# Trimming both ends of a tuned SwiGLU kernel: unread register setup, a one-column memset, 18 fillers for 20, and the last copy on ScalarE

## The chip, the cores and the metric

The kernel runs on one core of one Trainium2 chip. The metric is the device time of one execution in microseconds (us), lower is better. A run counts as slow when it is over 1.5% above the fastest run of the same kernel, and as fast otherwise; all quoted times are of fast runs unless a run is named as slow. The span in a profile is shorter than the time of the same run by 1.3 to 1.4 us; it counts from the first to the last recorded instruction.

## The reference

```python
B, S, D, F = 1, 2048, 640, 1536          # bf16 everywhere
def reference(x, w_gate, w_up, w_down):
    g = _silu(x @ w_gate)
    u = x @ w_up
    return (g * u) @ w_down
```

## The kernel before

The kernel cuts the 2048 rows into four blocks of 512. For each block it computes gate and up projections (tiles pg and pu) for 12 column groups, multiplies, and then computes the down projection in two tiles per 128 rows: po_a (512 columns) and po_b (128 columns). For the first block, x is loaded row by row and transposed on TensorE; the other blocks are loaded already transposed by DMA. While the first loads are under way, TensorE runs matmuls on a tile of ones whose result nobody reads. These are the "fillers"; they are meant to keep TensorE busy so that its clock goes to full rate early (how far these runs show it is asked under e4).

The head, with cuts marked:

```python
    ones = consts.tile([P, P], bf16)
    nc.vector.memset(ones[:], 1.0)
    queues = (nc.sync, nc.scalar)
    halves = ((0, KD // 2 + 1), (KD // 2 + 1, KD))
    for c in (0, 1):                      # x rows: chunks 0, 1 from SP, 2, 3 from ACT
        for i, eng in enumerate(queues):
            load_x(eng, c + 2 * i, c + 2 * i + 1)
    for dst, src in ((wg_sb, wg_v), (wu_sb, wu_v)):   # first 128 columns of both weights
        for eng, (k0, k1) in zip(queues, halves):
            eng.dma_start(out=dst[:, k0:k1, wslice(0, 1)], in_=src[:, k0:k1, wslice(0, 1)])
    # ... the other weights, then transposing loads of the later blocks
                h = (SUB - 1) * P
                warm(N_WARM)                          # N_WARM = 20
                for n, c in enumerate((0, 2, 1)):     # the "third chunk" below is c = 1
                    transpose_chunk(c, [(nc.vector.tensor_copy, ("po_a", "po_b")[n % 2], 0, KD)])
                transpose_chunk(SUB - 1, [...])
                warm(2)
                proj(pg, wg_sb, fc, sb, 0, h)         # first gate projection, 384 columns
                proj(pg, wg_sb, fc, sb, h, S_BLK)
                proj(pu, wu_sb, fc, sb, 0, S_BLK)     # first up projection
```

The tail, for the last 128 rows:

```python
            nc.scalar.copy(ot[:, 0:DA], po_a[:])
            # ... if last:
                nc.sync.dma_start(out=out2[s0 : s0 + P, 0:DA], in_=ot[:, 0:DA])      # 128 KB
                nc.vector.tensor_copy(out=ot[:, DA:D], in_=po_b[:])
                nc.scalar.dma_start(out=out2[s0 : s0 + P, DA:D], in_=ot[:, DA:D])    # 32 KB
```

After tracing, a function `_trim` takes barrier instructions out of the program's first block.

Of the kernel before, what the change touches and what calls it, by code (L numbers as in the profile page):

```python
# [10 lines left out]
def _body(  # L11
# [8 lines left out]
    nc = tc.nc  # L20
    P = nc.NUM_PARTITIONS
    f32 = mybir.dt.float32
    bf16 = mybir.dt.bfloat16
    ACT = mybir.ActivationFunctionType
    ALU = mybir.AluOpType

    B, S0, D = x.shape
# [8 lines left out]
    NSB = S // S_BLK  # L36
    SUB = S_BLK // P
    DA = 512
    N_WARM = 20
    W_CHUNKS = [(0, 1), (1, 3), (3, 6), (6, 9), (9, 12)]  # L40
    assert D % P == 0 and F % P == 0 and S % S_BLK == 0 and D > DA and SUB >= 2

    consts = ctx.enter_context(tc.tile_pool(name="consts", bufs=1))
# [25 lines left out]
    def load_w(eng, dst, src, a, b):  # L69
        eng.dma_start(out=dst[:, :, wslice(a, b)], in_=src[:, :, wslice(a, b)])  # L70
# [1 line left out]
    def load_x(eng, c0, c1):  # L72
        eng.dma_start(out=x_sb[:, c0:c1, :], in_=x_v[:, c0:c1, :])

    ones = consts.tile([P, P], bf16)
    silu_first = consts.tile([P, 1], f32)
    nc.vector.memset(ones[:], 1.0)  # L77

# [6 lines left out]
        for eng, (k0, k1) in zip(queues, halves):  # L85
            eng.dma_start(out=dst[:, k0:k1, wslice(0, 1)], in_=src[:, k0:k1, wslice(0, 1)])
    load_w(nc.sync, wg_sb, wg_v, *W_CHUNKS[1])
    nc.scalar.activation(silu_first[:], ones[:, 0:1], ACT.Silu)  # L88
    load_w(nc.sync, wu_sb, wu_v, *W_CHUNKS[1])
    for a, b in W_CHUNKS[2:]:  # L90
        load_w(nc.sync, wg_sb, wg_v, a, b)
# [6 lines left out]
    pw = psum.tile([P, S_BLK], f32, tag="gu", name="pw", bufs=4)  # L98

    def warm(n):  # L100
        for _ in range(n):
            nc.tensor.matmul(  # L102
                pw[:, 0:P], lhsT=ones[:], rhs=ones[:], start=True, stop=True
            )

    def keep_order(engine):
# [12 lines left out]
    def transpose_chunk(c, parts):  # L119
        c_sl = slice(c * P, (c + 1) * P)  # L120
        for copy, tag, k0, k1 in parts:
            pt = psum.tile([P, k1 - k0, P], bf16, tag=tag, name="pt")
            for kd in range(k0, k1):
                nc.tensor.transpose(  # L124
                    out=pt[:, kd - k0, :],
                    in_=x_sb[:, c, kd * P : (kd + 1) * P],
                    identity=ident[:],
                )
            copy(out=xT[:, k0:k1, c_sl], in_=pt[:])  # L129

    def proj(ps, w_sb, fc, sb, c0, c1):
        for kd in range(KD):
            nc.tensor.matmul(  # L133
                ps[:, c0:c1],
                lhsT=w_sb[:, kd, fc * P : (fc + 1) * P],
                rhs=xT[:, kd, sb * S_BLK + c0 : sb * S_BLK + c1],
                start=(kd == 0),
                stop=(kd == KD - 1),
            )

    for sb in range(NSB):
        s_sl = slice(sb * S_BLK, (sb + 1) * S_BLK)
        for fc in range(KF):
            pg = psum.tile([P, S_BLK], f32, tag="gu", name="pg", bufs=4)
            pu = psum.tile([P, S_BLK], f32, tag="gu", name="pu", bufs=4)
            if sb == 0 and fc == 0:
                h = (SUB - 1) * P
                warm(N_WARM)
                for n, c in enumerate((0, 2, 1)):
                    transpose_chunk(  # L150
                        c, [(nc.vector.tensor_copy, ("po_a", "po_b")[n % 2], 0, KD)]
                    )
                transpose_chunk(
                    SUB - 1,
                    [
                        (nc.vector.tensor_copy, "po_b", 0, 2),
                        (nc.scalar.copy, "po_a", 2, KD),
                    ],
                )
                warm(2)  # L160
                proj(pg, wg_sb, fc, sb, 0, h)
                proj(pg, wg_sb, fc, sb, h, S_BLK)
                proj(pu, wu_sb, fc, sb, 0, S_BLK)
                keep_order(mybir.EngineType.PE)
                keep_order(mybir.EngineType.Activation)
            else:
                proj(pg, wg_sb, fc, sb, 0, S_BLK)
                proj(pu, wu_sb, fc, sb, 0, S_BLK)
            sg = work.tile([P, S_BLK], f32)
            nc.scalar.activation(sg[:], pg[:], ACT.Silu)  # L170
            nc.vector.tensor_tensor(  # L171
                out=aT[:, fc, s_sl], in0=sg[:], in1=pu[:], op=ALU.mult
            )

        for j in range(SUB):
            s0 = sb * S_BLK + j * P
            last = sb == NSB - 1 and j == SUB - 1
            po_a = psum.tile([P, DA], f32, tag="po_a", name="po_a")
            for kf in range(KF):
                nc.tensor.matmul(  # L180
                    po_a[:],
                    lhsT=aT[:, kf, s0 : s0 + P],
                    rhs=wd_sb[:, kf, 0:DA],
                    start=(kf == 0),
                    stop=(kf == KF - 1),
                )
            po_b = psum.tile([P, D - DA], f32, tag="po_b", name="po_b")
            for kf in range(KF):
                nc.tensor.matmul(  # L189
                    po_b[:],  # L190
                    lhsT=aT[:, kf, s0 : s0 + P],
                    rhs=wd_sb[:, kf, DA:D],
                    start=(kf == 0),
                    stop=(kf == KF - 1),
                )
            ot = outp.tile([P, D], bf16)
            nc.scalar.copy(ot[:, 0:DA], po_a[:])  # L197
            if not last:
                nc.scalar.copy(ot[:, DA:D], po_b[:])  # L199
                nc.sync.dma_start(out=out2[s0 : s0 + P, :], in_=ot[:])  # L200
            else:
                nc.sync.dma_start(out=out2[s0 : s0 + P, 0:DA], in_=ot[:, 0:DA])
                nc.vector.tensor_copy(out=ot[:, DA:D], in_=po_b[:])  # L203
                nc.scalar.dma_start(out=out2[s0 : s0 + P, DA:D], in_=ot[:, DA:D])


def _trim(nc):







    blocks = nc.main_func.blocks
    main, end = blocks[0], blocks[-1]

    def of_barrier(ins):
        s = ins.sync_info
        if s is None:  # L220
            return isinstance(ins, mybir.InstDrain) and not ins.is_reset_sema
        names = [w.ant_name for w in s.on_wait] + [u.ant_name for u in s.on_update]
        return bool(names) and all(n.startswith("barrier_") for n in names)

    main.instructions[:] = [i for i in main.instructions if not of_barrier(i)]

    raised = {}
    for n, block in enumerate(blocks):
        for k, ins in enumerate(block.instructions):
            s = ins.sync_info  # L230
            for u in s.on_update if s is not None else []:
                raised[u.id] = (n, k)
    closing = []
    for ins in end.instructions:
        if of_barrier(ins):
            continue
        s = ins.sync_info
        if isinstance(ins, mybir.InstDrain) and s is not None and s.on_wait:
            waits = sorted(s.on_wait, key=lambda w: raised[w.id], reverse=True)
            closing.append(  # L240
                mybir.InstDrain(
                    name=ins.name,
                    engine=ins.engine,
                    is_reset_sema=ins.is_reset_sema,
                    debug=ins.debug,
                    sync_info=mybir.SyncInfo(on_wait=waits, on_update=list(s.on_update)),
                )
            )
        elif isinstance(ins, mybir.InstDrain) and ins.is_reset_sema:
            closing.append(  # L250
                mybir.InstDrain(
                    name=ins.name,
                    engine=mybir.EngineType.SP,
                    is_reset_sema=True,
                    reset_range_start=ins.reset_range_start,
                    reset_range_stop=ins.reset_range_stop,
                    debug=ins.debug,
                )
            )
        elif isinstance(ins, mybir.InstISA):  # L260
            closing.append(
                mybir.InstISA(
                    name=ins.name,
                    engine=mybir.EngineType.SP,
                    isa_opcode=ins.isa_opcode,
                    instr=list(ins.instr),
                    op_name=ins.op_name,
                    ant_dict=ins.ant_dict,
                    ant_isa_is_sequencer_only=ins.ant_isa_is_sequencer_only,
                    verify=ins.verify,  # L270
                    debug=ins.debug,
                    ins=[],
                    outs=[],
                )
            )
        else:
            closing.append(ins)
    end.instructions[:] = closing


def kernel(tc, *args):
    _body(tc, *args)
    tc.close()
    tc.compile()
    _trim(tc.nc)
# [30 lines left out]
```

## Time and profile before

| | before |
|---|---|
| time, median of 3 runs at first | 164.5 us (164.31 to 164.64) |
| span of the profiled run | 163.5 us |
| first gate projection starts | 5.08 us |
| first up projection starts | 6.54 us |
| TensorE's last signal to the end of the span | 2.08 us |

The first lines are from the page of the kernel before: the span, the busy time of each engine, and the chain of work that ended last, by engine.

```profile
span 163.5 us, 2138 instructions
PE 161.0 (98%) x911; PEld 81.3 (50%) x911; DVE 35.1 (21%) x54; ACT 44.0 (27%) x82; POOL 0.6 (0%) x6
...
PE 98%; DVE 0%; issue 0%; DVEq 0%
```

TensorE is busy 98% of the span and is 98% of the chain. What the change can reach are the few microseconds before the steady stream of matmuls and the two after it. The next lines are the timeline of the first 9 us of the same kernel. Columns: start, length, engine, source line, operation, output and inputs, number of instructions, and in brackets the idle time of the engine before it with what ended it. "PE" is a matmul on TensorE, "PEld" a weight load; further down "SPq" and "ACTq" are DMA issues.

```profile
start us, us, engine line op out<-in xcount [idle before <-releaser]
...
0.18 0.17 DVE L77 MEMSET ones<- 128x128 bf16 x1 [0.18 <-issue]
...
0.40 2.31 PE L102 MATMUL pw<-ones 128*128 128x128 bf16 x20 [0.40 <-DVE ones L77]
...
2.50 2.53 PE L124 MATMUL pt<-ident,x_sb 128*128 128x128 bf16 x20
...
3.28 1.02 DVE L129 COPY xT<-pt 128x640 bf16<-128x640 bf16 x2 [2.94 <-PE pt L124]
...
3.78 0.98 PEld L124 LDWEIGHTS <-x_sb 128*128 128x128 bf16 x10 [0.27 <-DMA x_sb<-in_x_dram]
...
4.54 0.69 DVE L129 COPY xT<-pt 128x640 bf16<-128x640 bf16 x2 [0.23 <-PE pt L124]
...
5.08 1.62 PE L133 MATMUL pg<-xT,wg_sb 128*128 128x384 bf16 x10
...
6.54 1.24 PE L133 MATMUL pu<-xT,wu_sb 128*128 128x512 bf16 x5
```

The reader should see three things. The fillers end where the transposes start, at 2.50. TensorE's weight load for the third x chunk waits 0.27 us for a DMA, until 3.78. The first gate projection starts at 5.08, just after the VectorE copy of the third chunk (the two copies from 4.54 on; the first of them ends near 5.03). The spacing of the 128x384 matmuls goes from 0.320 us to 0.163 us at 5.94: TensorE's clock goes from half rate to full rate there.

The DMA completions in the trace give the times at which the x chunks were there, in TensorE's order: 2.13, 2.62, 3.74 and 4.15 us. The first gate weights came in two halves, at 4.84 (SP) and 4.92 (ACT).

The tail of the same kernel, from the timeline:

```profile
160.80 0.58 ACT L197 CAST ot<-po_a 128x512 bf16<-128x512 f32 x1 [2.37 <-PE po_a L180]
161.41 0.33 SPq L202 DMA_DIRECT2D out_dram<-ot  x1
161.48 0.29 DVE L203 CAST ot<-po_b 128x128 bf16<-128x128 f32 x1 [12.34 <-PE po_b L189]
161.80 0.37 ACTq L204 DMA_DIRECT2D out_dram<-ot  x1
```

TensorE's last signal was at 161.40. VectorE starts the last copy 0.08 us later, and the last store is issued 0.40 us after the signal. It lands at 163.30, 1.50 us after its issue.

### The profile page before, as it was taken

The numbers are of one execution on the slowest core, as the hardware profiler recorded it, in microseconds if no ns is written. First come the engines' busy times: TensorE is split into PE (matmuls) and PEld (weight loads), VectorE is DVE, ScalarE is ACT, GpSimd is POOL, SyncE is SP. The second block draws the span as 40 slices with busy tenths as digits, with TensorE's granted clock in tenths as the row PEclk, the third lists the DMA queues.
The fourth block names the chain that finished last, engine by engine and source line by source line (L and its number), as shares of the span: only waits on it lengthen the run. The fifth ranks groups of instructions, "written<-read, shape, count | busy, mean of one in ns | idle before, by whom it ended". The sixth has DMA issues, their size and how long they took to land.

```text
span 163.5 us, 2138 instructions
## 1 busy us (share of the span) xinstructions
PE 161.0 (98%) x911; PEld 81.3 (50%) x911; DVE 35.1 (21%) x54; ACT 44.0 (27%) x82; POOL 0.6 (0%) x6
## 2 busy tenths in 40 slices
PE   9999999999999999999999999999999999999994
PEld 8644444455544444455554444445564444445552
DVE  2223333300013333310003333330001333331000
ACT  3222222222322222222232222222233222222321
POOL 1000000000000000000000000000000000000000
DMA  7999999611110000001210000001111000000112
GB/s 222 261 335 331 363 250 196 131 40 44 40 40 0 0 4 0 0 2 40 71 53 0 0 2 0 0 4 40 40 40 40 4 0 0 0 0 0 44 48 73
DMA packets 18953, 11.27 MB, mean 69 GB/s; under 512 B 9728, under 2 KB 18944, under 8 KB 18944
## 3 DMA queue, kind: packets, MB, share of 16 engines
q1 hardware_dynamic: 17968, 10.65, 23.1%
q10 hardware_dynamic: 976, 0.49, 1.1%
q8 instruction: 7, 0.11, 0.3%
q14 instruction: 2, 0.02, 0.0%
HBM read 6.55 MB, written 2.62 MB: 56 GB/s over the span
## 4 chain that ended last, share of the span: by engine, by line
PE 98%; DVE 0%; issue 0%; DVEq 0%
PE pg L133 32%; PE pu L133 32%; PE po_a L180 25%; PE po_b L189 7%; PE pw L102 2%; PE pt L124 1%; DVE ot L203 0%; DVE ones L77 0%; DVEq L203 0%
## 5 line engine op out<-in xcount | busy, mean ns | idle before, releaser
L133 PE MATMUL pg<-xT,wg_sb 128*128 128x512 bf16 (+2 forms) x245 | 60.0, 377 | 0.0
L133 PE MATMUL pu<-xT,wu_sb 128*128 128x512 bf16 x240 | 59.6, 379 | 0.0
L171 DVE TENSOR_TENSOR aT<-sg,pu 128x512 bf16<-128x512 f32 x48 | 33.0, 687 | 110.9 <-PE pu L133 110.9
L170 ACT ACTIVATE sg<-pg 128x512 f32<-128x512 f32 x48 | 28.7, 597 | 72.3 <-PE pg L133 72.3
L180 PE MATMUL po_a<-wd_sb,aT 128*128 128x512 bf16 x192 | 44.0, 379 | 0.0
L133 PEld LDWEIGHTS <-wg_sb 128*128 128x128 bf16 x245 | 23.9, 98 | 27.6 <-issue 0.3
L133 PEld LDWEIGHTS <-wu_sb 128*128 128x128 bf16 x240 | 23.4, 98 | 28.1
L180 PEld LDWEIGHTS <-aT 128*128 128x128 bf16 x192 | 18.3, 98 | 19.8
L197 ACT CAST ot<-po_a 128x512 bf16<-128x512 f32 x16 | 9.4, 585 | 40.4 <-PE po_a L180 40.4
L189 PEld LDWEIGHTS <-aT 128*128 128x128 bf16 x192 | 12.1, 98 | 3.8
L189 PE MATMUL po_b<-wd_sb,aT 128*128 128x128 bf16 x192 | 13.3, 219 | 0.0
L199 ACT CAST ot<-po_b 128x128 bf16<-128x128 f32 x15 | 4.0, 265 | 1.1
L102 PE MATMUL pw<-ones 128*128 128x128 bf16 x22 | 2.7, 313 | 0.4 <-DVE ones L77 0.4
L203 DVE CAST ot<-po_b 128x128 bf16<-128x128 f32 x1 | 0.3, 291 | 12.3 <-PE po_b L189 12.3
L124 PE MATMUL pt<-ident,x_sb 128*128 128x128 bf16 x20 | 2.5, 313 | 0.0
L102 PEld LDWEIGHTS <-ones 128*128 128x128 bf16 x22 | 2.3, 147 | 0.4 <-DVE ones L77 0.4
L129 DVE COPY xT<-pt 128x640 bf16<-128x640 bf16 (+1 forms) x4 | 1.7, 439 | 3.2 <-PE pt L124 3.2
L124 PEld LDWEIGHTS <-x_sb 128*128 128x128 bf16 x20 | 2.1, 146 | 0.3 <-DMA x_sb<-in_x_dram 0.3
L88 ACT ACT_TABLE_LOAD x1 | 1.3, 1283 | 2.0 <-issue 2.0
L129 ACT COPY xT<-pt 128x384 bf16<-128x384 bf16 x1 | 0.5, 478 | 1.5 <-PE pt L124 1.5
masks.py:199 POOL TENSOR_SCALAR_AFFINE_SELECT ident<-ident 128x128 bf16<-128x128 bf16 x1 | 0.3, 292 | 0.1
L88 ACT ACTIVATE silu_first<-ones 128x1 f32<-128x1 bf16 x1 | 0.2, 203 | 0.0
(6 smaller groups left out, 0.8 us busy)
## 6 DMA issues: line engine op xcount, KB each, us to landing
out_dram<-ot SPq DMA_DIRECT2D x15, 160.0 KB, 1.8
wd_sb<-in_w_down_dram SPq DMA_DIRECT2D x1, 1920.0 KB, 11.4
wg_sb<-in_w_gate_dram SPq DMA_DIRECT2D x3, 480.0 KB, 7.5
wu_sb<-in_w_up_dram SPq DMA_DIRECT2D x3, 480.0 KB, 7.6
x_sb<-in_x_dram SPq DMA_DIRECT2D x2, 160.0 KB, 2.7
x_sb<-in_x_dram ACTq DMA_DIRECT2D x2, 160.0 KB, 3.0
wg_sb<-in_w_gate_dram SPq DMA_DIRECT2D x1, 320.0 KB, 4.6
wu_sb<-in_w_up_dram SPq DMA_DIRECT2D x1, 320.0 KB, 5.1
```

The costliest lines, as they stand in the source:

```text
L88: nc.scalar.activation(silu_first[:], ones[:, 0:1], ACT.Silu)
L102: nc.tensor.matmul(pw[:, 0:P], lhsT=ones[:], rhs=ones[:], start=True, stop=True)
L124: nc.tensor.transpose(out=pt[:, kd - k0, :], in_=x_sb[:, c, kd * P : (kd + 1) * P], identity=ident[:],)
L129: copy(out=xT[:, k0:k1, c_sl], in_=pt[:])
L133: nc.tensor.matmul(ps[:, c0:c1], lhsT=w_sb[:, kd, fc * P : (fc + 1) * P], rhs=xT[:, kd, sb * S_BLK + c0 : sb * S_BLK + c1], start=(kd == 0 ...
L170: nc.scalar.activation(sg[:], pg[:], ACT.Silu)
L171: nc.vector.tensor_tensor(out=aT[:, fc, s_sl], in0=sg[:], in1=pu[:], op=ALU.mult)
L180: nc.tensor.matmul(po_a[:], lhsT=aT[:, kf, s0 : s0 + P], rhs=wd_sb[:, kf, 0:DA], start=(kf == 0), stop=(kf == KF - 1),)
L189: nc.tensor.matmul(po_b[:], lhsT=aT[:, kf, s0 : s0 + P], rhs=wd_sb[:, kf, DA:D], start=(kf == 0), stop=(kf == KF - 1),)
L197: nc.scalar.copy(ot[:, 0:DA], po_a[:])
L199: nc.scalar.copy(ot[:, DA:D], po_b[:])
L203: nc.vector.tensor_copy(out=ot[:, DA:D], in_=po_b[:])
```

## The change

The intent: let TensorE start earlier, because register moves whose value nobody reads no longer run ahead of the first memset on TensorE and VectorE, and the memset itself becomes short (one column, which the fillers then read 128 times over, with stride 0); take two fillers out, because the start is earlier; and let the last copy and its store sit on one engine.

```diff
@@ -36,7 +36,7 @@
     NSB = S // S_BLK
     SUB = S_BLK // P
     DA = 512
-    N_WARM = 20
+    N_WARM = 18
     W_CHUNKS = [(0, 1), (1, 3), (3, 6), (6, 9), (9, 12)]
     assert D % P == 0 and F % P == 0 and S % S_BLK == 0 and D > DA and SUB >= 2
 
@@ -72,7 +72,8 @@
     def load_x(eng, c0, c1):
         eng.dma_start(out=x_sb[:, c0:c1, :], in_=x_v[:, c0:c1, :])
 
-    ones = consts.tile([P, P], bf16)
+    ones = consts.tile([P, 1], bf16)
+    ones_p = ones[:].to_broadcast([P, P])
     silu_first = consts.tile([P, 1], f32)
     nc.vector.memset(ones[:], 1.0)
 
@@ -85,7 +86,7 @@
         for eng, (k0, k1) in zip(queues, halves):
             eng.dma_start(out=dst[:, k0:k1, wslice(0, 1)], in_=src[:, k0:k1, wslice(0, 1)])
     load_w(nc.sync, wg_sb, wg_v, *W_CHUNKS[1])
-    nc.scalar.activation(silu_first[:], ones[:, 0:1], ACT.Silu)
+    nc.scalar.activation(silu_first[:], ones[:], ACT.Silu)
     load_w(nc.sync, wu_sb, wu_v, *W_CHUNKS[1])
     for a, b in W_CHUNKS[2:]:
         load_w(nc.sync, wg_sb, wg_v, a, b)
@@ -100,7 +101,7 @@
     def warm(n):
         for _ in range(n):
             nc.tensor.matmul(
-                pw[:, 0:P], lhsT=ones[:], rhs=ones[:], start=True, stop=True
+                pw[:, 0:P], lhsT=ones_p, rhs=ones_p, start=True, stop=True
             )
 
     def keep_order(engine):
@@ -200,7 +201,7 @@
                 nc.sync.dma_start(out=out2[s0 : s0 + P, :], in_=ot[:])
             else:
                 nc.sync.dma_start(out=out2[s0 : s0 + P, 0:DA], in_=ot[:, 0:DA])
-                nc.vector.tensor_copy(out=ot[:, DA:D], in_=po_b[:])
+                nc.scalar.copy(ot[:, DA:D], po_b[:])
                 nc.scalar.dma_start(out=out2[s0 : s0 + P, DA:D], in_=ot[:, DA:D])
 
 
@@ -222,7 +223,23 @@
         names = [w.ant_name for w in s.on_wait] + [u.ant_name for u in s.on_update]
         return bool(names) and all(n.startswith("barrier_") for n in names)
 
-    main.instructions[:] = [i for i in main.instructions if not of_barrier(i)]
+
+    read = {
+        (i.engine, r) for b in blocks for i in b.instructions for r in i.regs_accessed()[0]
+    }
+    bare = (mybir.EngineType.PE, mybir.EngineType.DVE)
+
+    def idle_register(ins):
+        writes = ins.regs_accessed()[1]
+        return (
+            ins.engine in bare
+            and bool(writes)
+            and not any((ins.engine, r) in read for r in writes)
+        )
+
+    main.instructions[:] = [
+        i for i in main.instructions if not of_barrier(i) and not idle_register(i)
+    ]
 
     raised = {}
     for n, block in enumerate(blocks):
```

## The prediction

> **What bounds the kernel.** TensorE. The page gives PE 98% of a 163.5 us span; the chain of work that ended last is PE 98%, with everything else about 2%. The steady part (4 blocks of pg, pu, po_a, po_b) is not touched by the change. It can act only on the first 5 us and on the last 2 us.
>
> **Head, from the timeline of the first 7 us.** The VectorE memset of `ones` runs 0.18 to 0.34 us (165 ns). The first filler starts at 0.40; 20 fillers go about 107 ns apart; the first transpose starts at 2.50. The x chunks land (DMA completions) at 2.13, 2.62, 3.74 and 4.15 us in the order in which TensorE wants them. So TensorE does 10 transposes, sits idle 0.27 us until 3.78 (in the waits: weight load of x_sb on DMA), and only then goes on: the second half of the transposes, the last copies, the first real projection at 5.08. Chunk three's landing, not the fillers, sets 5.08. The clock gate opens inside the first projections: 128x384 matmuls are 320 ns apart at 5.36 and 163 ns from 5.94.
>
> **The change, part by part.**
> 1. Register setup. The two built programs, compared engine by engine, have no register move on TensorE or VectorE in either: the build already drops them. Apart from the memset the engines' preambles are the same. Gain 0.
> 2. One-column memset. Estimate from the trace: POOL's one-column memsets take 98 ns against 204 ns for 128x128, so VectorE's 165 ns may fall to about 70 to 100. The first filler starts near 0.30, 0.07 to 0.10 us earlier. Stride-0 reads of ones: I expect the same 107 ns spacing.
> 3. 18 fillers for 20: 2 x 107 = 0.21 us less. With 2 the first transpose starts near 2.2 instead of 2.50, just behind the chunk's landing at 2.13. The 10 transposes end 0.3 us earlier and the idle time before chunk three grows from 0.27 to about 0.55 us. First projection still at about 5.1. Gain about 0.
> 4. Last copy. Before: TensorE signals at 161.40, VectorE starts 80 ns later, takes 291, the ACT-issued store goes at 161.80 and lands at 163.30, closing the program. ScalarE is free at 161.39 and does this shape in 265 ns, starting about 67 ns after the signal (as its po_a copy did), and the store follows on the same engine. The store moves about 0.04 us earlier. Three waits of VectorE leave the program as well, off the path.
>
> **On the critical path:** 0.04 us in the tail, 0 to 0.1 us in the head.
>
> **The clock gate.** The Trainium skill, "TensorE: Matmul & The Clock Gate", Part 1, says that the half-rate state ends after a sustained busy window of about 3.4 us, free-running, so that the point varies from run to run. The trace agrees in kind: spacing halves 5.4 us after TensorE's first work. An earlier start shifts this by at most 0.1 us, worth half of that; random phase can move single runs by several tenths, about the scatter of before (164.31 to 164.64). The longer gap could delay the opening by a window, about 1.7 us lost (my estimate: half of 3.4); I give that 5%.
>
> **Prediction:** 164.4 us, range 164.0 to 164.8; within 2% nearly certain.
>
> **What would show it.** First filler near 0.30; spacing 107; first transpose near 2.2; idle before chunk three near 0.55 us; first projection within 0.2 us of 5.08; last ScalarE copy 265 ns; store issue about 0.35 us after TensorE's last signal instead of 0.40.
>
> **What would make it wrong.** Stride-0 operands read slower; the gate opening a window earlier or later; chunk three landing at another time, because TensorE no longer sets it but the queues do; the build dropping registers differently on the chip.

## The result, and the profile after

| | before | after |
|---|---|---|
| time, median | 164.57 us (164.31 to 164.93, 6 runs) | 164.79 us (164.49 to 165.13, 6 runs) |
| ratio of the fast runs | | 1.001, 95% interval 0.9991 to 1.003 |
| profiled span | 163.5 us | 163.6 us |
| first gate projection starts | 5.08 us | 5.60 us |
| first up projection starts | 6.54 us | 6.68 us |
| last signal to the end | 2.08 us | 2.09 us |

A ratio here is the mean time of one kernel's fast runs over the mean of the other's in the same rounds, so it is not quite the ratio of the medians. The two kernels cannot be told apart by time. The page after:

```profile
span 163.6 us, 2131 instructions
PE 160.1 (98%) x909; PEld 80.2 (49%) x909; DVE 34.8 (21%) x53; ACT 44.3 (27%) x83; POOL 0.6 (0%) x6
...
PE 96%; DMA 2%; DVE 0%; SPq 0%; ACT 0%; issue 0%
PE pg L134 32%; PE pu L134 32%; PE po_a L181 25%; PE po_b L190 7%; DMA x_sb<-in_x_dram 2%; DVE xT L130 0%; PE pt L125 0%; SPq L73 0%; ACT ot L204 0%
```

A DMA has entered the chain with 2%. The same places of the timeline as before:

```profile
0.15 0.06 DVE L78 MEMSET ones<- 128x1 bf16 x1 [0.15 <-issue]
...
0.30 2.10 PE L103 MATMUL pw<-ones 128*128 128x128 bf16 x18 [0.30 <-DVE ones L78]
...
2.50 1.25 PE L125 MATMUL pt<-ident,x_sb 128*128 128x128 bf16 x10
...
3.25 1.03 DVE L130 COPY xT<-pt 128x640 bf16<-128x640 bf16 x2 [3.04 <-PE pt L125]
...
4.56 0.73 PE L125 MATMUL pt<-ident,x_sb 128*128 128x128 bf16 x10 [0.81 <-DMA x_sb<-in_x_dram]
...
5.05 0.69 DVE L130 COPY xT<-pt 128x640 bf16<-128x640 bf16 x2 [0.77 <-PE pt L125]
...
5.60 1.25 PE L134 MATMUL pg<-xT,wg_sb 128*128 128x384 bf16 x10 [0.19 <-DVE xT L130]
...
6.68 1.24 PE L134 MATMUL pu<-xT,wu_sb 128*128 128x512 bf16 x5
```

And the part of the chain of waits, in order of time, that shows why (start, length, what):

```profile
0.45 4.06 DMA x_sb<-in_x_dram
...
4.56 0.47 PE pt L125 x5
...
5.60 1.25 PE pg L134 x10
```

The memset fell from 0.17 to 0.06 us and the first filler came at 0.30 instead of 0.40, as intended. Nothing came of it. The transposes started at 2.50 again, now held by the landing of the first chunk (2.45) and not by the fillers. The third chunk's load landed at 4.51, so TensorE sat idle for 0.81 us (1.13 us from one transpose to the next), and the first gate projection started 0.52 us later than in the profile of before. It then took only 1.09 us instead of 1.46, because the clock had already gone to full rate by 4.6 us. The sum, 0.52 - 0.37 = 0.14 us (rounded from the trace), is the whole difference at the first up projection.

The tail after:

```profile
160.94 0.59 ACT L198 CAST ot<-po_a 128x512 bf16<-128x512 f32 x1 [2.37 <-PE po_a L181]
161.55 0.33 SPq L203 DMA_DIRECT2D out_dram<-ot  x1
161.56 0.27 ACT L204 CAST ot<-po_b 128x128 bf16<-128x128 f32 x1
161.86 0.37 ACTq L205 DMA_DIRECT2D out_dram<-ot  x1
```

TensorE's last signal was at 161.54. The copy now starts 0.02 us after it and the store is issued 0.32 us after it, so 0.08 us earlier than before. Yet the end comes 2.09 us after the signal, against 2.08.

The three parts add up exactly in the two profiles: from the start of the first up projection to TensorE's last signal both take 154.858 us. So 163.48 = 6.54 + 154.86 + 2.08 and 163.63 = 6.68 + 154.86 + 2.09. The change does nothing in the middle; what it did at the two ends is what the experiments are about.

### The profile page after: what moved, and what is told of

The parts are those of the page before. It is cut to its first block, busy times and chain, and to the rows that moved or that the text cites. A ratio compares the mean times of both kernels' runs of the same rounds, so it can differ in the third digit from the quotient of the medians.

```text
span 163.6 us, 2131 instructions
## 1 busy us (share of the span) xinstructions
PE 160.1 (98%) x909; PEld 80.2 (49%) x909; DVE 34.8 (21%) x53; ACT 44.3 (27%) x83; POOL 0.6 (0%) x6
## 4 chain that ended last, share of the span: by engine, by line
PE 96%; DMA 2%; DVE 0%; SPq 0%; ACT 0%; issue 0%
PE pg L134 32%; PE pu L134 32%; PE po_a L181 25%; PE po_b L190 7%; DMA x_sb<-in_x_dram 2%; DVE xT L130 0%; PE pt L125 0%; SPq L73 0%; ACT ot L204 0%
## 5 line engine op out<-in xcount | busy, mean ns | idle before, releaser
L125 PE MATMUL pt<-ident,x_sb 128*128 128x128 bf16 x20 | 2.0, 266 | 0.9 <-DMA x_sb<-in_x_dram 0.8
L125 PEld LDWEIGHTS <-x_sb 128*128 128x128 bf16 x20 | 1.5, 120 | 1.4 <-DMA x_sb<-in_x_dram 1.4
```

Source lines behind the costliest of these rows:

```text
L125: nc.tensor.transpose(out=pt[:, kd - k0, :], in_=x_sb[:, c, kd * P : (kd + 1) * P], identity=ident[:],)
```

## The experiments

Theory: (1) the register edit removes nothing; (2) the head is set by when x chunks and first weights land and by when the clock opens, both of which differ from run to run and neither of which the change touches; (3) the tail gains a few hundredths of a microsecond at most. Rivals: the earlier start or the missing fillers cost something (a later clock); the change has a cost of its own of about 0.2 us; and for the tail, that ScalarE is in its own way.

Runs e1 to e4 were on one chip together, e5 to e8 on another, e9 to e11 on a third. Each group is compared with its own runs of the kernel before (of those with e9 to e11 one, 166.85 us, was slow and is not counted).

### e1_registers_only: the register edit alone

```diff
 (kernel before)
+    main.instructions[:] = [
+        i for i in main.instructions if not of_barrier(i) and not idle_register(i)
+    ]
```

> Only the register edit. The built program is the same as the kernel before's but for debug lines, so this is a run of before against itself. Theory (the register edit removes nothing): ratio 1.000, within 0.2% either way, memset at about 0.18 us and first filler at about 0.40 us; the spread of this ratio is the noise that every other ratio here has to beat. Rival (the edit removes register moves that the trace does not show): the memset starts clearly before 0.15 us and the time falls by 0.1 us or more.

Measured: 164.46 us (164.05 to 164.79, 6 runs) against 164.68 (164.23 to 165.42, 11 runs) of before; ratio 0.9985, interval 0.9961 to 1.0009. The built program is that of before, instruction for instruction: neither has a register move on TensorE or VectorE left, since the build drops them itself. In the profile the first filler is at 0.398 us, as in before. TensorE's timeline of this run:

```profile
0.40 2.31 PE L102 MATMUL pw<-ones 128*128 128x128 bf16 x20 [0.40 <-DVE ones L77]
2.50 1.94 PE L124 MATMUL pt<-ident,x_sb 128*128 128x128 bf16 x20
...
4.71 1.25 PE L133 MATMUL pg<-xT,wg_sb 128*128 128x384 bf16 x10 [0.16 <-DVE xT L129]
```

There is no wait for the third chunk: it landed at 3.46. The clock was at full rate from 3.57 us on, and the first up projection started at 5.80 us (its record is missing; this is the next one's 6.02 less one spacing of 0.216). That is 0.74 us earlier than in the other profile of the very same program. What follows: two profiles of one program differ at this point by more than the change was ever going to give, and a ratio of 0.15% off 1 with these counts is noise. The rival is out: the memset started no earlier.

### e2_tail_only: only the last copy on ScalarE

```diff
 (kernel before)
-                nc.vector.tensor_copy(out=ot[:, DA:D], in_=po_b[:])
+                nc.scalar.copy(ot[:, DA:D], po_b[:])
```

> Only the last copy on ScalarE. Theory: from the end of TensorE's last signal to the issue of the last store 0.40 us falls to 0.35 us or a little less, time -0.04 us, so ratio 0.9998, not to be told from 1. Rival (ScalarE is still busy with the po_a copy and delays it): the copy starts more than 0.1 us after the signal and the store leaves no earlier than before.

Measured: 164.74 us (164.35 to 165.05), ratio 0.9995, interval 0.997 to 1.0019. In the trace the copy starts 0.023 us after the signal and the store is issued 0.318 us after it, instead of 0.401. The gain at the issue is 0.08 us, twice the forecast. But the store landed 1.89 us after the signal, as before (1.90), and the span ended 2.06 us after it (2.08 before). The rival, that ScalarE delays the copy, is out. Where the 0.08 us went is asked in e9 to e11.

### e3_head_only: only the memset, the stride-0 ones and the 18 fillers

```diff
 (kernel before)
-    N_WARM = 20
+    N_WARM = 18
-    ones = consts.tile([P, P], bf16)
+    ones = consts.tile([P, 1], bf16)
+    ones_p = ones[:].to_broadcast([P, P])
 (and lhsT=ones_p, rhs=ones_p in warm)
```

> Only the one-column memset, stride-0 ones and 18 fillers. Theory (the landing of the x chunks and of the first gate weights sets the first projection, the fillers do not): first filler near 0.30, first projection between 5.0 and 5.7 us depending on when the last part of the third chunk lands, ratio 1.000 within 0.2%. Rival (fewer fillers open TensorE's clock later, which is what cost the 0.2 us): full-rate spacing is reached later than 5.9 us and the ratio is 1.001 to 1.005.

Measured: 164.76 us (164.38 to 166.32, 6 runs), ratio 1.0011, interval 0.9976 to 1.0046; one run of 166.32 makes the interval wide. In the profile the fillers run at the same 0.107 us spacing, the third chunk landed at 4.04, the first gate projection started at 5.38 and took 1.09 us; full-rate spacing was reached by 4.9 us. The rival said later than 5.9: in this it is wrong, and of the six other profiles with 18 fillers and the same head only e9 opens that late (table below). The theory's window for the start (5.0 to 5.7) holds.

### e4_no_fillers: the changed kernel with no filler ahead of the transposes

```diff
-                warm(N_WARM)
```

> The changed kernel without any filler ahead of the transposes. Theory (fillers do not gate the first projection, they only open the clock): first projection still between 5.0 and 5.7 us, but half-rate spacing lasts about 1 to 3 us longer, 0.5 to 1.5 us more in all (ratio 1.003 to 1.009). Rival (fillers are in the way of the transposes): the first projection comes earlier and the time falls. Rival 2 (fillers are useless, the transposes alone open the clock at the same point): ratio 1.000.

Measured: 165.13 us (164.46 to 166.13, 6 runs), ratio 1.0029, interval 0.9995 to 1.0063. TensorE's timeline:

```profile
2.46 2.32 PE L125 MATMUL pt<-ident,x_sb 128*128 128x128 bf16 x20 [2.46 <-DMA x_sb<-in_x_dram]
...
4.83 1.80 PE L134 MATMUL pg<-xT,wg_sb 128*128 128x384 bf16 x10
6.46 1.24 PE L134 MATMUL pu<-xT,wu_sb 128*128 128x512 bf16 x5
```

The first gate projection started at 4.83 us, a little before the theory's 5.0 to 5.7. Other profiles with fillers reach 4.71 to 4.94, so taking the fillers away does not bring it forward beyond them. It took 1.64 us instead of 1.09, because the clock opened only at about 6.0 us. The runs spread over 1.7 us, against 0.7 us in e1. The mean loss of 0.3% is in the direction of the theory, but the interval just includes none. So the fillers do not hold the start. That they do their work through the clock is not shown: with 20 fillers the clock opened at 5.94, 3.57 and 6.46 us, so 6.0 without any is inside what fillers give too, and what they are worth is not settled by these six runs and one profile.

### e5_fillers_40: the changed kernel with 40 fillers

```diff
-    N_WARM = 18
+    N_WARM = 40
```

> The changed kernel with 40 fillers ahead of the transposes. Theory (there is slack of about 1 us between the end of 18 fillers and the landing of the third chunk; beyond it fillers are on the path): the fillers run to about 4.0 to 4.6 us, the first projection starts at 5.3 to 6.5 instead of 4.7 to 5.6, most of the projections run at full rate from the start, so the time changes by +0.2 to +1.0 us (ratio 1.001 to 1.006). Rival (fillers are hidden however many): ratio 1.000, first projection at about 5.0.

Measured: 165.51 us (165.2 to 166.22, 4 runs), ratio 1.0054, interval 1.0032 to 1.0076.

```profile
0.31 4.10 PE L103 MATMUL pw<-ones 128*128 128x128 bf16 x40 [0.31 <-DVE ones L78]
4.25 1.35 PE L125 MATMUL pt<-ident,x_sb 128*128 128x128 bf16 x20
...
6.07 1.25 PE L134 MATMUL pg<-xT,wg_sb 128*128 128x384 bf16 x10 [0.35 <-DVE xT L130]
```

The transposes start at 4.25 instead of 2.5, the first gate projection at 6.07, as forecast. The 22 more fillers are on the path for part of their length. So there is a slack after 18 fillers, of the order of the wait for the third chunk, and it is not endless. Two fillers fewer, 0.21 us, lie inside that slack.

### e7_weights_before_x3: another order of the first loads

```diff
-    for c in (0, 1):
-        for i, eng in enumerate(queues):
-            load_x(eng, c + 2 * i, c + 2 * i + 1)
+    for eng, c in ((nc.sync, 0), (nc.scalar, 2), (nc.sync, 1)):
+        load_x(eng, c, c + 1)
 (first gate weights as before)
+        if n == 0:
+            load_x(nc.scalar, 3, 4)
 (the transposes of chunk 3 moved behind the first 384 columns of the gate projection,
  and the first up projection split into the same two parts)
```

> The changed kernel with the last x chunk issued behind the first gate weights and transposed after the first gate projection of 384 columns; the first up projection is split the same way. Theory (the first projection waits for DMA bandwidth: four x chunks and the first gate weights, 800 KB): 160 KB less ahead of it, so the first projection starts at about 4.4 to 4.7 instead of 4.7 to 5.6, and the second column of work ends 0 to 0.5 us earlier; ratio 0.997 to 1.000. Rival (a late part of one DMA engine sets it whatever the order): first projection no earlier than 5.0, ratio 1.000 or above for the extra instructions.

Measured: 165.18 us (164.5 to 166.56, 6 runs), ratio 1.004, interval 1.0006 to 1.0073: slower by 0.4%, and the expectation failed. The waits of TensorE (engine, line, what it waited for: us in total, times, longest):

```profile
...
PEld L135 <- DMA wg_sb<-in_w_gate_dram: 0.9, 1, 0.9
```

ACT's half of the first gate weights landed at 3.82 us, but SP's half landed at 5.31, later than the 4.5 to 4.9 of every other profile. The likely reason, not tested, is that SP's half still stands behind two x chunks in SP's queue, and that the moved chunk on ACT now shares the bandwidth with it. This order was a poor test of the bandwidth idea: if that is so, it took bytes from ahead of one half and put them beside the other. It does show that the first gate weights can hold the first projection as well as the third x chunk.

### e8_after_again: the changed kernel once more

No edit.

> The changed kernel itself once more. Theory (its 0.2 us over before was chance: the landing of the x chunks and the opening of the clock differ from run to run): ratio 0.998 to 1.001, the first up projection starts anywhere from 5.8 to 6.8 us, and from there to TensorE's last signal it takes 154.86 us as in every run so far. Rival (the change has a cost of its own): ratio 1.001 again or above.

Measured: 164.71 us (164.6 to 164.87, 5 runs), ratio 1.0001, interval 0.9987 to 1.0014. The 0.1% of the first measurement did not come back. One part of the expectation failed: from the first up projection (6.05 us, again one spacing ahead of the first record) to the last signal it took 155.29 us, not 154.86. The waits show where:

```profile
...
PEld L134 <- DMA wg_sb<-in_w_gate_dram: 1.1, 2, 0.8
...
PE pg L134 <- DMA wg_sb<-in_w_gate_dram: 0.3, 1, 0.3
```

With the first column group done early, TensorE stood 0.42 us before the second group, whose gate weights had not landed. The same stretch is longer in three more of the early ones, by 0.05 us in e6, 0.24 in e10 and 0.09 in e11, but not in e1. So behind the third x chunk and the first weights a third DMA is waiting to take over. An early first projection is then worth less than it seems.

### e6_tail_five_copies: is the last copy on the path?

```diff
-                nc.scalar.copy(ot[:, DA:D], po_b[:])
+                for _ in range(5):
+                    nc.scalar.copy(ot[:, DA:D], po_b[:])
```

> The changed kernel with the last 128x128 copy done five times over on ScalarE before its store (same result). Theory (the last copy is on the path one for one): four more copies of 0.265 us put the store 1.06 us later and the time rises by about 1.1 us, ratio 1.0065. Rival (the tail is set by the other store, or by the end of the program): less than half of that.

Measured: 165.65 us (165.54 to 166.04, 4 runs), ratio 1.0061, interval 1.0044 to 1.0077; e8 on the same chip had 164.71.

```profile
161.01 1.46 ACT L205 CAST ot<-po_b 128x128 bf16<-128x128 f32 x5
162.50 0.36 ACTq L206 DMA_DIRECT2D out_dram<-ot  x1
```

The store was issued 1.51 us after the signal instead of 0.32, so 1.19 us later, and the end came 3.16 us after the signal instead of 2.09: 1.07 us later. The copy is on the path, but 0.12 us of the delay cost nothing. That was the first hint that in the changed kernel the last store waits for something else for about a tenth of a microsecond.

### e9_no_big_store and e10_no_big_store_vector: what the last store waits for

Both give a wrong result: the 128 KB store of the last tile is left out.

```diff
 (e9: changed kernel)
-                nc.sync.dma_start(out=out2[s0 : s0 + P, 0:DA], in_=ot[:, 0:DA])
 (e10: also)
-                nc.scalar.copy(ot[:, DA:D], po_b[:])
+                nc.vector.tensor_copy(out=ot[:, DA:D], in_=po_b[:])
```

> Wrong result on purpose: the changed kernel without the 128 KB store of the last tile's first 512 columns. So far the last store was issued 0.08 us earlier with the copy on ScalarE (0.319 after TensorE's last signal against 0.401) but landed no earlier (1.89 to 1.91 against 1.90). Theory A (the last store's parts queue behind the 128 KB store on the same DMA engines, whose landing is 1.71 to 1.74 either way): without that store the last store lands about 1.5 us after its issue, 1.80 after the signal, and the program ends at about 1.98 instead of 2.06 to 2.11. Theory B (a store issued by ScalarE right after its own copy takes longer by itself): it still lands at about 1.9 and the end stays at 2.06 to 2.11.

> The same wrong-result kernel with the last copy on VectorE. Theory A: issue at 0.40, landing 1.88 to 1.90, end at about 2.06 to 2.08, so 0.08 later than with ScalarE: without the big store the earlier issue does count. Theory B: the same end as e9_no_big_store within 0.03 us.

The tails, e9 first and then e10 (start, length, engine and line, operation):

```profile
161.66 0.27 ACT L203 CAST ot<-po_b 128x128 bf16<-128x128 f32 x1
161.95 0.37 ACTq L204 DMA_DIRECT2D out_dram<-ot  x1
```

```profile
161.20 0.29 DVE L203 CAST ot<-po_b 128x128 bf16<-128x128 f32 x1 [12.34 <-PE po_b L190]
161.52 0.37 ACTq L204 DMA_DIRECT2D out_dram<-ot  x1
```

The trace's records of signals and DMA completions, all in us after TensorE's last signal:

| kernel | last copy on | last store issued | it landed | after its issue | 128 KB store landed | end |
|---|---|---|---|---|---|---|
| before | VectorE | 0.401 | 1.901 | 1.500 | 1.714 | 2.082 |
| e1, e3 | VectorE | 0.401, 0.402 | 1.897, 1.902 | 1.496, 1.500 | 1.710, 1.711 | 2.078, 2.078 |
| after | ScalarE | 0.319 | 1.908 | 1.589 | 1.737 | 2.088 |
| e2, e8 | ScalarE | 0.318, 0.319 | 1.891, 1.924 | 1.573, 1.605 | 1.720, 1.752 | 2.062, 2.094 |
| e9 | ScalarE | 0.317 | 1.808 | 1.491 | none | 1.989 |
| e10 | VectorE | 0.402 | 1.896 | 1.494 | none | 2.078 |

Without the big store the earlier issue counts in full: 1.989 against 2.078, 0.09 us. With it, the last store lands about 0.17 to 0.19 us after the big one whether it was issued at 0.32 or at 0.40. Theory A of the expectation holds, theory B does not. In the kernel before, the last store came just late enough not to be held at all (1.500 against 1.494 without the big store). The Trainium skill, "DMA: Bandwidth & Descriptors", section "Issuing engines are not separate DMA queues", says that transfers started from different engines run on the same 16 DMA engines and interleave. The table fits it: the last store, issued from another queue, is delayed by the big one by about 0.1 us here (1.573 to 1.605 after the issue against 1.491).

The times of these two kernels, 164.69 and 164.61 us with two runs each (ratios 1.0001 and 0.9996), decide nothing.

### e11_split_po_a: getting the big store out of the way

```diff
-            nc.scalar.copy(ot[:, 0:DA], po_a[:])
+            if not last:
+                nc.scalar.copy(ot[:, 0:DA], po_a[:])
+            else:
+                nc.scalar.copy(ot[:, 0 : DA // 2], po_a[:, 0 : DA // 2])
+                nc.vector.tensor_copy(out=ot[:, DA // 2 : DA], in_=po_a[:, DA // 2 : DA])
```

> Right result: the changed kernel with the last tile's 512-column copy split between ScalarE and VectorE, so that the 128 KB store is issued 0.15 to 0.25 us earlier. Theory A: the big store lands 0.15 to 0.25 us earlier, the last store no longer queues behind it, lands at about 1.80 after the signal, the end comes at about 1.98 instead of 2.08: 0.1 us, which the times (interval 0.15 to 0.25%) cannot resolve, ratio 0.9985 to 1.001. Theory B: the end stays at 2.06 to 2.11.

Measured: 164.98 us (164.78 to 165.35, 6 runs), ratio 1.0023, interval 1.0 to 1.0046. The edit did not do what it was for:

```profile
160.45 0.37 ACT L201 CAST ot<-po_a 128x256 bf16<-128x256 f32 x1 [2.37 <-PE po_a L181]
160.85 0.42 DVE L202 CAST ot<-po_a 128x256 bf16<-128x256 f32 x1 [12.06 <-ACT ot L201]
161.07 0.27 ACT L208 CAST ot<-po_b 128x128 bf16<-128x128 f32 x1 [0.25 <-PE po_b L190]
161.30 0.33 SPq L207 DMA_DIRECT2D out_dram<-ot  x1
161.37 0.37 ACTq L209 DMA_DIRECT2D out_dram<-ot  x1
```

The two half copies ran one after the other, because the program makes VectorE wait for ScalarE's copy into the same tile. The big store was therefore issued 0.25 us after the signal, 0.25 us later than before, while the last store was issued at 0.319 as in the changed kernel. The end moved from 2.09 to 2.34 us, by the same 0.25. So the run is a test of theory A after all, in the other direction: the big store moved, the last store's issue did not, and the end followed the big store. Its time missed the forecast too (0.9985 to 1.001), on the slow side. No version here beats both kernels; a version that gets the big store out earlier would gain about the 0.09 us of e9 (an estimate), less than these times can resolve.

### The head in the runs that leave its order alone

All profiles but e5 (40 fillers) and e7 (another order). Times in us from the start of the span. "1st" in the last column but one is the time from the first gate projection to the first up projection.

| profile | third x chunk landed | first gate weights, SP half | first gate projection | 1st takes | full rate seen from |
|---|---|---|---|---|---|
| before | 3.74 | 4.84 | 5.08 | 1.46 | 5.94 |
| e1 (same program) | 3.46 | 4.53 | 4.71 | 1.09 | 3.57 |
| e2 | 3.18 | 4.88 | 4.93 | 1.82 | 6.46 |
| after | 4.51 | 4.92 | 5.60 | 1.09 | 4.6 |
| e8 (same program) | 3.62 | 4.90 | 4.94 | 1.10 | 4.3 |
| e3 | 4.04 | 4.53 | 5.38 | 1.09 | 4.9 |
| e4 | 3.36 | 4.78 | 4.83 | 1.64 | 6.0 |
| e6 (head of after) | 3.65 | 4.61 | 4.99 | 1.09 | 4.6 |
| e9 (head of after) | 3.85 | 4.93 | 5.19 | 1.59 | 6.34 |
| e10 (head of after) | 3.33 | 4.68 | 4.85 | 1.17 | 5.09 |
| e11 (head of after) | 3.81 | 4.58 | 5.01 | 1.09 | 4.2 |

The first up projection starts at 5.80 to 6.74 us with the old head (three profiles, mean 6.36) and at 6.02 to 6.78 with the new one (seven, mean 6.31): no difference that these could show. Where the third chunk is late, the projection follows it by 1.1 to 1.35 us (five transposes and a VectorE copy), 1.1 when the transposes already run at full rate. Where it is early, the projection follows the gate weights by 0.05 us (e2; in e4 and e8 the weights and the third chunk's copy come within 0.01 us of each other) or the three VectorE copies, 0.49 us each, that queue behind one another (e1). None of these is shown to be something the change moves, with one doubt. The first x chunk landed at 2.13 to 2.36 us in the three profiles with 20 fillers and at 2.39 to 2.64 in the ten others, without overlap; because the groups were run on different chips, and on the one chip that had both the gap was only 0.03 to 0.12 us with two of each, whether the change has a part in it stays open.

## Why the prediction was right or wrong

- **Time.** 164.4 us with 164.0 to 164.8 was predicted, 164.79 measured, no difference from before. The range held by 0.01 us, with single runs from 164.49 to 165.13, so that it held at all is luck. The sign of the small forecast difference (0.1 to 0.2 us down) was not borne out, but with an interval of 0.2% on either side of the ratio its sign means nothing.
- **Register setup: right.** Gain 0; e1 is the same program.
- **Memset: right.** It took 59 ns, a little under the estimate of 70 to 100; the first filler came at 0.305 us, where 0.30 was predicted, and the spacing stayed 107 ns, so stride 0 cost nothing.
- **"With 2 the first transpose starts near 2.2": wrong.** It started at 2.50. The step took the landing of the first chunk, 2.13 us, from one profile as if it were fixed. It was 2.45 in the profile after, and between 2.13 and 2.64 in all of them. The two fillers dropped had been covering that time. The idle time before the third chunk, forecast at 0.55 us, was 0.81. Since the third chunk comes later still, the mistake cost the sum nothing.
- **"First projection still at about 5.1. Gain about 0": right in kind, wrong as a forecast of one run.** It was 5.60 in the profile after and 4.71 to 5.60 over the eleven profiles of the table. The text blamed the third chunk alone; e2 and e7 show the gate weights, e1 the VectorE copies, and e8 the next weights as next in line.
- **The clock: right that its phase varies; its effect was undersized and the worry did not come true.** The Trainium skill, "TensorE: Matmul & The Clock Gate", Part 1, says that the window is free-running and that the point of opening differs from run to run. The profiles agree: full rate from 3.57 to 6.46 us over the table, 3.57 and 5.94 for one and the same program; that is 3.2 to 6.1 us after TensorE's first work, the shortest (e1) a little under the 3.4 us that the prediction took from that page. The phase alone is up to 0.7 us of head (1.09 against 1.82), where the prediction had "several tenths". The forecast risk that a longer gap delays the opening did not show in the one profile after: the gap grew to 1.13 us and TensorE came out of it at full rate.
- **"The store moves about 0.04 us earlier" and "On the critical path: 0.04 us in the tail": the first was mis-sized, the second wrong.** The store's issue moved 0.08 us, because ScalarE began 0.02 us after the signal and not 0.067 (the delay of its po_a copy; why the two differ is not known). But the end did not move, because the last store lands behind the 128 KB store (e9, e10, e11). The step that failed is that of the store being the only thing that closes the program.

What stays open: why one of the sixteen parts of a load can come more than a microsecond after the others. In the profile after, fifteen parts of the third chunk had landed by 3.34 us and the last came at 4.51; nine of the x packets took over 250 ns, where most take 55. But the same kernel ran without it in e8 (last part at 3.62, fifteen by 3.33) and had ten such packets, so their number does not explain it. No experiment here was aimed at the cause.

## What to carry to other kernels

Before trimming the start of a kernel, look at which arrival the first real work waits for, in more than one profile: here instructions ahead of that arrival could be shortened by 0.3 us for nothing. Where two stores close a program, look at the landings and not at the issues: here moving the smaller one forward gained nothing, because it then landed behind the larger one. And run the unchanged program against itself first: here the first up projection of one program moved by 0.74 us between two profiles, more than the whole change could give.

## What the Trainium skill lacked or had wrong

- "TensorE: Matmul & The Clock Gate", Part 4, says that the full rate does not engage for transpose mode. Here transposes through an identity, built with the transpose flag, ran 56 ns apart at 4.63 to 5.07 us in the profile after, which is the full rate, and in e1 and e8 the rate went up in the middle of the transposes (at 3.57 and 4.26 us). In e4, with no filler, the clock opened 3.5 us after TensorE's first work, of which the first 2.1 us were transposes; this suggests that they count as activity, though one run does not prove it.
- "DMA: Bandwidth & Descriptors" says that transfers from different queues interleave. It gives no size for what the end of a program pays: here a 32 KB store issued 0.31 us after a 128 KB store landed about 0.1 us later than it does alone, and one issued 0.39 us after it within 0.01 us of its time alone.
- No page that I used has how soon an engine starts on TensorE's last signal: VectorE's copy began 0.078 to 0.080 us after it in four profiles, ScalarE's 0.022 to 0.024 us in the nine others, though ScalarE's po_a copy began 0.067 us after its own signal.
- "DMA: Bandwidth & Descriptors", section "Why a DMA increments its semaphore by 16 and not by 1", says that the up to 16 engines of a transfer finish independently. It does not say by how much: here the last of the 16 parts of a 160 KB load came from 0.003 to 1.18 us after the fifteenth.
